# Masks of the first half-sequence added in PSUM, wider idle products and a new order of loads and instructions, in an attention and swish kernel on one core

## The chip, the cores and the metric

The kernel runs on one NeuronCore of a Trainium2 chip. The metric is the device time of one execution in microseconds (us). Before the change the median of three runs is 231.59 us (231.52 to 231.60).

The core has five instruction streams: TensorE (PE in the profile, its weight loads PEld), VectorE (DVE), ScalarE (ACT), GpSimd (POOL) and SyncE (SP), which here only issues DMAs. TensorE writes to PSUM, eight banks of 512 float32 columns on 128 partitions; the other engines bring its results to SBUF.

## The reference

Attention with two kinds of heads, then a layer with w_in, a swish with a factor for each column, and w_out:

```python
rel = pos[:, None] - pos[None, :]
causal = rel >= 0
stream_keep = causal & ((pos[None, :] < 4) | ((rel >= 0) & (rel < 64)))
mask = where(is_retrieval, causal, stream_keep)        # by head
a = softmax(where(mask, q @ k.T / sqrt(64), -1e9))
x = (a @ v) laid out as [3072, 512]                    # 4 batches x 768 rows, 8 heads x 64
h = x @ w_in                                           # [512, 2048]
out = (h * sigmoid(beta * h)) @ w_out                  # [2048, 512]
```

q, k and v are [4, 8, 768, 64] in float32. Heads 0, 2 and 6 are retrieval heads (causal), the others streaming heads (a window of 64 keys and the first 4 keys, the sinks). Inputs are cast to bf16 on the core.

## The kernel before, in words

**Units.** The work is cut into eight half-sequences ("halves") of NQ = 384 rows, two to a batch, numbered n = 0 to 7. Each goes through these stages, whose names are those in the profile:

- q and k are loaded as float32 (tiles `q2f`, `k2f`, 192 KB for a pair of heads; from half 4 on `wf`), cast to bf16 (`c`), transposed on TensorE through `ident` (`b<-ident,c`; six transposes for a pair and half, from half 4 on by DMA) and copied to `QK`. A load of this kind is called a tile below.
- v is loaded in three parts (`vf`, 256 KB each), cast to `vb` and shifted by 64 rows to `vs`.
- Scores go to a PSUM tile `sp` (two tiles of two banks, one step of two heads each); ScalarE takes exp of a whole step to `es` (for two steps of half 0 to a borrowed tile `osb`).
- Masks: after exp, VectorE or GpSimd multiplies `es` by `mask_c` (the causal triangle) or `mask_s` (the streaming window), both 0 or 1.
- Sums (`b<-es,two` and others), their reciprocal, a spread over the partitions (`b<-sc,sel`), the products with V (`sp<-es,vb` and `vs`), and the normalized `xT`, the transposed x.
- w_in: 16 column blocks of 128 for each half, four 384-column products each (`b<-xT,w_in`); ScalarE's tanh to `t`, VectorE's `gT`.
- w_out: three row blocks of 128 for each half, 16 512-column products each (`b<-w_out,gT`), planned in groups of three; copied to `osb` and stored.

w_in and w_out are loaded in four transfers of 1 MB each, through the same three `wf` buffers; each is cast by four casts on GpSimd, one for each column block of w_in or each 128 rows of w_out. `KP` holds keys of the streaming heads gathered from `QK`, nine copies for each half from half 2 on.

**Order.** Nothing is left to a scheduler. `add` (line 137) enters each step, with what it needs and what PSUM banks it takes; the number of a step is its place in the order of these calls. `SEQUENCE` (line 41) lists the step numbers, `CHOICE` (line 97) names the engine of each step that has a choice. `run` (line 147) walks through `SEQUENCE`, works out a planned start from the costs written beside each step, gives each step that takes a buffer the slot that came free first, and emits the steps sorted by planned start. The engines run their instructions in the order of emission and wait on semaphores for one another, so the costs set an order and no time. All instructions are issued from one helper, so the profile gives line 121 for nearly all of them; groups are told apart by tile and shape.

**Idle products.** `FILLS` (line 107) names steps ahead of which TensorE multiplies a cleared operand, or transposes `ident`, that many times (`fill`, line 555) into the bank which the step overwrites; `fill_first` issues 25 at the start. In the profile they are `b<-xT`, `sp<-xT` and `b<-ident`, 128 columns each; there are 25 + 34.

**Loads.** SyncE issues nearly all DMAs in order on one queue. The order before, up to the third transfer of w_out (q0 is the q tile of pair 0; the half stands in brackets; [0] k0 comes from ScalarE's queue; in w_in and w_out the four transfers are numbered 0 to 3):

```
[0] q0 k3 q3 q1 k1 q2, beta, [1] q0 k0, [0] k2, [0] V2 V0 V1, w_in 0, [1] k2 q2 q3 q1 k1 k3,
w_in 1, w_in 2, [1] V0 V1 V2, [2] q1, w_in 3, w_out 3, [2] k1 k2 q0 q2 k0 q3 k3,
w_out 0, w_out 1, [3] k0, w_out 2, [3] q2 k3 q1, [2] V, ...
```

Of the kernel before, what the change touches and what calls it, by code (L numbers as in the profile page):

```python
# [19 lines left out]
NQ = 384  # L20
# [75 lines left out]
]  # L96
CHOICE = (
    "daagaddadadddadaddaddgggdgdddgaaagaggggdaagdddaddadaagddddgaaddgddaaadagdddaddagggggadggdgdgggdgggad"
    "gaadaadaaaadaaaaadaddddaadda"
# [7 lines left out]
FILLS = {28: 8, 45: 5, 32: 1, 51: 7, 36: 1, 54: 5, 60: 1, 24: 4, 76: 2}  # L107
# [19 lines left out]
class _Plan:  # L127

    LAT = {"pe": 0.2, "act": 0.2, "dve": 0.22, "pool": 0.2, "sp": 0.0}

    def __init__(self, rings):
        self.free = {k: [(0.0, i) for i in range(n)] for k, n in rings.items()}
        self.ops, self.refs, self.log, self.where = [], {}, [], {}
        self.same = {}

    def add(self, eng, cost, f, needs=(), gives=(), take=(), drop=(), dma=0.0, mode=None, port=False, begun=(), lat=None, parts=1):

        needs = dict.fromkeys(m for n in needs for m in self.same.get(n, [n]))  # L140
        one = isinstance(eng, str)
        alts = [(eng, cost)] if one else list(zip(eng, cost))
        self.ops.append((0, len(self.ops), dict(alts), (lambda e: f()) if one else f, tuple(needs), tuple(gives),
                         tuple(take), tuple(drop), dma, mode, port, tuple(begun),
                         lat or (2.0 if dma > 0.2 else 3.2), parts))

    def run(self):

        done = {}
        now = {e: 0.0 for o in self.ops for e in o[2]}  # L150
        mode = None
        bus, lock = 1.1, 0.0
# [1303 lines left out]
```

## Time and profile before

| | |
|---|---|
| median of three runs | 231.59 us (231.52 to 231.60) |
| profiled execution: span from the first to the last instruction | 229.49 us |
| granted TensorE clock | 0.999 |
| instructions | 6530 |
| DMA traffic | 42.28 MB, 84264 packets, 66042 of them under 512 B |

The profile is of one execution; it gives the span and no other time for it, so the 2.1 us between span and median are what lies around the instructions. The page has the engines' busy time, the span in 40 slices (busy tenths), the DMA queues, the chain that ended last, the costliest groups and the DMA issues. Lines of the timeline read: start, length, engine, line, operation, tile written and tiles read, shape, count, and in brackets the engine's idle time ahead of it and what ended it. A busy TensorE is not a TensorE at its peak: a row's length holds the pipeline's latency once, so the distance between products is (length - length of one)/(count - 1).

### The profile page before, as it was taken

To read this page: it belongs to the slowest core of one execution; us is meant where nothing else is said; L and a number is where in the kernel's file an instruction comes from. 1 tells how busy PE (TensorE), PEld (TensorE's weight loads), DVE (VectorE), ACT (ScalarE), POOL (GpSimd) and SP (SyncE) were. 2 spreads that over 40 slices of the span, in tenths; PEclk is the share of its full clock that TensorE was granted. 3 is DMA by queue.
4 is the path that set the end of the run, shared out by engine and by line. 5 is a ranking of instruction groups with operands and counts; after the bars stand their busy time and mean duration, and the time that the engine had idled before them with its cause. 6 is when DMAs were issued, how large, how long until landed. Compare 5 with 4: busy or idle time off the path is not lost.

```text
span 229.5 us, 6530 instructions
## 1 busy us (share of the span) xinstructions
PE 222.0 (97%) x2589; PEld 126.8 (55%) x2589; DVE 159.3 (69%) x394; ACT 140.8 (61%) x233; POOL 94.2 (41%) x236
## 2 busy tenths in 40 slices
PE   7699999999999999999999999999999999999995
PEld 6465466664544555464654555745655555456543
DVE  4697988888588957984686687793596459167621
ACT  5799979896076378726894188526857357018610
POOL 5428956964966307559265563048200000000000
PEclk9999999999999999999999999999999999999999
DMA  6999999999989979999999985977300106321012
GB/s 187 274 321 362 237 321 340 375 341 226 220 192 252 213 158 229 270 172 213 250 233 203 209 197 167 192 146 149 101 3 0 50 2 181 105 91 46 3 46 91
DMA packets 84264, 42.28 MB, mean 184 GB/s; under 512 B 66042, under 2 KB 77002, under 8 KB 84234
## 3 DMA queue, kind: packets, MB, share of 16 engines
q1 hardware_dynamic: 83962, 41.67, 74.3%
q8 instruction: 20, 0.33, 0.6%
q10 hardware_dynamic: 272, 0.20, 0.3%
q14 instruction: 10, 0.08, 0.1%
HBM read 32.27 MB, written 6.37 MB: 168 GB/s over the span
## 4 chain that ended last, share of the span: by engine, by line
PE 84%; DMA 4%; ACT 4%; DVE 4%; SPq 1%; issue 1%; ACTq 0%; DVEq 0%
PE b L121 74%; PE sp L121 10%; DMA k2f<-in_k_dram 2%; DMA q2f<-in_q_dram 2%; DVE KP L121 2%; DVE es L121 1%; ACT QK L121 1%; ACT es L121 1%; DVE gT L121 1%; ACT osb L121 1%; SPq L121 1%; ACT c L121 1%; ACT t L121 0%; DVE xT L121 0%; DVE c L121 0%
## 5 line engine op out<-in xcount | busy, mean ns | idle before, releaser
L121 DVE SCALAR_TENSOR_TENSOR gT<-t,b 128x384 bf16<-128x384 f32 x128 | 68.8, 550 | 32.2 <-ACT t L121 28.0
L121 PE MATMUL b<-xT,w_in 128*128 128x384 bf16 x512 | 90.2, 326 | 0.2
L121 PE MATMUL b<-w_out,gT 128*128 128x512 bf16 (+2 forms) x400 | 89.0, 371 | 0.1
L121 ACT ACTIVATE t<-b,beta_h 128x384 f32<-128x384 f32 x128 | 73.0, 585 | 25.1 <-PE b L121 13.7
L121 PEld LDWEIGHTS <-w_in 128*128 128x128 bf16 x512 | 48.7, 98 | 33.9 <-POOL w_in L121 0.6
L121 PEld LDWEIGHTS <-gT 128*128 128x128 bf16 x400 | 37.0, 98 | 40.7 <-issue 1.0
L121 ACT ACTIVATE es<-sp 128x1024 bf16<-128x1024 f32 (+4 forms) x50 | 46.0, 952 | 7.0 <-PE sp L121 7.0
L121 ACT ACTIVATE osb<-b 128x512 f32<-128x512 f32 (+1 forms) x15 | 8.7, 578 | 39.3 <-PE b L121 39.3
L121 POOL CAST c<-wf 128x256 bf16<-128x256 f32 x48 | 18.6, 425 | 12.8 <-DMA wf<-in_k_dram 11.7
L121 POOL COPY KP<-QK 128x24 bf16<-128x24 bf16 (+5 forms) x41 | 9.8, 282 | 22.5 <-DMA QK<-c 13.5
L121 PE MATMUL sp<-QK 64*64 64x64 bf16 (+7 forms) x432 | 16.9, 234 | 1.1 <-ACT QK L121 0.8
L121 DVE TENSOR_SCALAR osb<-b 128x512 f32<-128x512 f32 (+1 forms) x10 | 6.7, 674 | 15.1 <-PE b L121 15.0
L121 DVE TENSOR_TENSOR xT<-sp,R 64x384 bf16<-64x384 f32 (+4 forms) x30 | 16.0, 554 | 1.6 <-PE sp L121 1.0
L121 PEld LDWEIGHTS <-QK 64*64 64x64 bf16 (+1 forms) x432 | 10.9, 105 | 9.8 <-issue 7.4
L121 DVE TENSOR_TENSOR es<-es,mask_c 128x128 bf16<-128x128 bf16 (+3 forms) x42 | 11.9, 308 | 4.2 <-ACT es L121 4.1
L121 DVE TENSOR_TENSOR es<-es,mask_s 128x128 bf16<-128x128 bf16 (+8 forms) x34 | 13.3, 417 | 0.9 <-ACT es L121 0.8
L121 PE MATMUL sp<-es,vb 128*64 128x64 bf16 (+5 forms) x245 | 13.3, 234 | 0.0
L121 POOL CAST vb<-wf 128x512 bf16<-128x512 f32 x18 | 10.8, 611 | 5.9 <-DMA wf<-in_v_dram 5.4
L121 PEld LDWEIGHTS <-vb 128*64 128x64 bf16 x257 | 11.4, 111 | 0.7
L121 DVE COPY QK<-b 128x384 bf16<-128x384 bf16 (+1 forms) x13 | 8.6, 671 | 3.8 <-PE b L121 3.8
L121 POOL COPY vs<-vb 64x512 bf16<-64x512 bf16 x19 | 11.1, 616 | 0.3
L121 POOL CAST w_out<-wf 128x512 bf16<-128x512 f32 x16 | 9.3, 613 | 3.5 <-DMA wf<-in_moe_w_out_dram 3.5
(112 smaller groups left out, 200.4 us busy)
## 6 DMA issues: line engine op xcount, KB each, us to landing
out_dram<-osb SPq DMA_DIRECT2D x23, 256.0 KB, 4.2
wf<-in_v_dram SPq DMA_DIRECT2D x18, 256.0 KB, 4.5
wf<-in_moe_w_in_dram SPq DMA_DIRECT2D x4, 1024.0 KB, 8.4
wf<-in_moe_w_out_dram SPq DMA_DIRECT2D x4, 1024.0 KB
R<-rd SPq DMA_DIRECT2D x9, 384.0 KB, 5.5
q2f<-in_q_dram SPq DMA_DIRECT2D x16, 192.0 KB, 4.5
wf<-in_q_dram SPq DMA_DIRECT2D x12, 256.0 KB, 4.0
wf<-in_k_dram SPq DMA_DIRECT2D x12, 256.0 KB, 4.1
```

Of the source, the lines that this page charges most:

```text
L121: ins = f(*a, **k)
```

## The change

It has these parts:

- For half 0 the masks after exp are gone (`masks_of` gives none). `scores` starts each PSUM bank with products of `ident` and a tile that holds 0 where a score is kept and -1e30 where not (`off_c`, 128 columns, from `mask_c`; `off_s`, 384 columns, from `mask_s`), and the score products add to it. In half 0 that is nine products of 128 columns and five of 384. The two tiles lie in the buffer of the first `xT`, beside the cleared operand, and VectorE forms them with one `tensor_scalar` each. `mask_c` is now made in a step of its own.
- `fill` issues pieces of up to 512 columns, with the cleared operand's first column repeated as moving operand; `FILLS` has four entries, with 16 units of 128 columns instead of 34, beside the 25 of `fill_first`.
- The first transfer of w_in is loaded in two halves, and its four casts may run on VectorE or ScalarE; two are given to VectorE.
- `SEQUENCE` and `CHOICE` are new; steps are emitted in the order of `SEQUENCE` itself, with no planned time, and the PSUM banks come from a list, `SLOTS`.

```diff
-FILLS = {28: 8, 45: 5, 32: 1, 51: 7, 36: 1, 54: 5, 60: 1, 24: 4, 76: 2}
+FILLS = {28: 6, 36: 1, 38: 1, 45: 8}
...
+    def const_off(dst, src):
+        dve.tensor_scalar(out=dst, in0=src, scalar1=-1.0, scalar2=1e30, op0=ADD, op1=MULT)
...
     def fill(dst):
-        for _ in range(held["fill"]):
-            if dst.dtype == BF16:
+        n = held["fill"]
+        if dst.dtype == BF16:
+            for _ in range(n):
                 pe.transpose(dst, ident, ident)
-            else:
-                pe.matmul(dst, blank, blank, start=True, stop=True)
+            return
+        while n:
+            w = min(n, 4)
+            pe.matmul(dst[:, 0:128 * w], blank, blank[:, 0:1].to_broadcast([128, 128 * w]), start=True, stop=True)
+            n -= w
...
+        for i, half in enumerate(rounds[ri] if x.n == 0 else []):
+            if half is None or half[0][0] == "k":
+                continue
+            at = [(0, off_s)] if half[0][0] == "w" else [(c, off_c) for (_, h, kb, c, q0, _) in half if kb * 128 == q0]
+            for j, (c, m) in enumerate(at):
+                pe.matmul(ps[:, i, c:c + m.shape[1]], ident, m, start=j == 0, stop=False, skip_group_check=True)
...
-                    pe.matmul(o[j][0], o[j][1], o[j][2], start=True, stop=True)
+                    pe.matmul(o[j][0], o[j][1], o[j][2], start=x.n > 0, stop=True, skip_group_check=x.n == 0)
...
     def masks_of(pi, ri, n):
         u = n % 2
+        if n == 0:
+            return []
...
-            add("sp", 0.5, lambda s=s, ld=ld: ld(s), dma=2.9, lat=2.1, gives=[("wf", w, s)], begun=[("begun", w, s)],
-                take=[("wf", (w, s), 4)])
+            halves = 2 if (w, s) == ("i", 0) else 1
+            for p in range(halves):
+                add("sp", 0.5, lambda s=s, ld=ld, a=((p, halves) if halves > 1 else ()): ld(s, *a), dma=2.9 / halves, lat=2.1, gives=[("wf", w, s, p)],
+                    needs=[("begun", w, s)] if p else [], begun=[] if p else [("begun", w, s)], take=[] if p else [("wf", (w, s), 4)])
```

The new order of the loads, decoded from `SEQUENCE` in the same notation:

```
beta, [0] q0 q2, [1] k0 q0, [0] q1 k1 k3 q3 k2, [0] V0, [1] q3, [0] V1, [1] k3, [0] V2, [1] q2 q1 k2, w_in 0a,
[1] k1, w_in 0b, w_in 1, [1] V1, w_in 2, [1] V2 V0, [2] q3 q0 q2 k0 k3, w_in 3, [2] k2 q1 k1, [3] q3, w_out 3,
[3] k1 q1, w_out 0, [3] q2 k0 k3 q0, w_out 1, w_out 2, [2] V, ...
```

On TensorE the scores of half 1 come earlier among those of half 0; the transposes of half 2 stand between the last w_in column blocks of half 0 instead of behind them; three of the four transpose steps of half 3 stand before the fourth group of w_out products of half 0; from half 5's w_in on, TensorE's list is the one of before. The `KP` copies of halves 2 and 3 move from VectorE to GpSimd, and the edge masks (`const_edges`) to GpSimd's start.

More of the change, by code (lines that the diff above doesn't have):

```diff
@@ L41 @@
 SEQUENCE = [
[54 rows of a table removed]
[51 rows of a table added]
 ]
 CHOICE = (
[L98 to L99 removed]
+    "aadaagddgdgddaddaaaddgdgaadaggdgaaddaddddaadddddgddddaadddddaaagaddadaagagdddgagdgaddgggdgggagdddggd"
+    "dadadddddadadaddaddddaadda"
+)
+SLOTS = (
+    "0123002131002301021301101023010213101023011030120103210311020312301201103201320132013201012302310120"
+    "1101023011001203120312031102030113102101023010231023102013012100110231002310231023101023201032100131"
+    "02103120013021303012131021023032013201320110321032103210321023023"
 )
@@ L127 @@
 class _Plan:
-    LAT = {"pe": 0.2, "act": 0.2, "dve": 0.22, "pool": 0.2, "sp": 0.0}
     def __init__(self, rings):
-        self.free = {k: [(0.0, i) for i in range(n)] for k, n in rings.items()}
-        self.ops, self.refs, self.log, self.where = [], {}, [], {}
-        self.same = {}
+        self.rings = rings
+        self.ops, self.where, self.same = [], {}, {}
     def add(self, eng, cost, f, needs=(), gives=(), take=(), drop=(), dma=0.0, mode=None, port=False, begun=(), lat=None, parts=1):
@@ L143, in add @@
         self.ops.append((0, len(self.ops), dict(alts), (lambda e: f()) if one else f, tuple(needs), tuple(gives),
-                         tuple(take), tuple(drop), dma, mode, port, tuple(begun),
-                         lat or (2.0 if dma > 0.2 else 3.2), parts))
+                         tuple(take), tuple(drop), dma, mode, port, tuple(begun), lat, parts))
     def run(self):
[L149 to L152, printed above, removed]
@@ L201, in run @@
-        return [x[1:] for x in sorted(order, key=lambda x: x[:2])]
+        choice = iter(CHOICE)
+        engine = {o[1]: {"a": "act", "d": "dve", "g": "pool"}[next(choice)] if len(o[2]) > 1 else list(o[2])[0] for o in self.ops}
+        slots = iter(SLOTS)
+        done, held = set(), {}
+        left = {}
+        assert sorted(SEQUENCE) == list(range(len(self.ops)))
+        for i in SEQUENCE:
+            _, _, _, f, needs, gives, take, drop, *_, begun, _, _ = self.ops[i]
+            assert done.issuperset(needs), (i, set(needs) - done)
+            done.update(gives)
+            done.update(begun)
+            for r, name, refs in take:
+                if r in ("b", "sp"):
+                    slot = r, int(next(slots))
+                    assert slot not in held, (i, slot, held[slot])
+                    held[slot] = name
+                    self.where[r, name] = slot[1]
+                    left[r, name] = refs
+            for key in drop:
+                if key in left:
+                    left[key] -= 1
+                    if not left[key]:
+                        del held[key[0], self.where[key]]
+            yield i, f, engine[i]
@@ L277 @@
     low = consts.tile([128, 1], F32, name="low")
-    blank = xp.tile([128, NP, NQ], BF16, name="xT")[:, 0, 0:128]
+    early = xp.tile([128, NP, NQ], BF16, name="xT")
+    blank, off_s, off_c = early[:, 0, 0:128], early[:, 1, :], early[:, 2, 0:128]
     one = consts.tile([128, 63], BF16, name="one")
@@ L496, in sink_rows @@
         t = bank((2 * b, "k"))
-        fill(t[:, 0:128])
+        fill(t)
         pe.matmul(t[0:96, :], sink_sel, v_b[b][:, 0, :, :].rearrange("p h d -> p (h d)"), start=True, stop=True)
@@ L518, with load_w_in @@
     wst = {}
-    def load_w_in(s):
-        f = stg.tile([128, 2048], F32, name="wf", bufs=RINGS["wf"]).rearrange("p (a n) -> p a n", a=NP)
-        sp.dma_start(out=f, in_=bass.AP(moe_w_in.tensor, moe_w_in.offset + s * 2 * FS, [[d_ff, 128], [128 * d_ff, NP], [1, 2 * FS]]))
-        wst["i", s] = f
+    def load_w_in(s, part=0, parts=1):
+        if part == 0:
+            wst["i", s] = stg.tile([128, 2048], F32, name="wf", bufs=RINGS["wf"]).rearrange("p (a n) -> p a n", a=NP)
+        n = 2 * FS // parts
+        sp.dma_start(out=wst["i", s][:, :, part * n:(part + 1) * n],
+                     in_=bass.AP(moe_w_in.tensor, moe_w_in.offset + s * 2 * FS + part * n, [[d_ff, 128], [128 * d_ff, NP], [1, n]]))
     def load_w_out(s):
@@ L711, in scores @@
         if x.n == 0:
-            fill(ps[:, 0, 0:128])
+            fill(ps[:, 0])
         ops = [[], []]
@@ L881, in sums @@
             if x.n == 0:
-                fill(x.sm[:, 0:128])
+                fill(x.sm)
         byj = [[] for _ in range(TU)]
@@ L1014, in pv @@
         if x.n == 0:
-            fill(o[:, 0, 0:128])
+            fill(o[:, 0])
         ops = [[], []]
@@ L1260, in attention @@
                     drop += [("k2f", (n, "d"))] if ri else []
+                if n == 0:
+                    needs += [("const", "ident")] + [("const", "off" + ("s" if h[0][0] == "w" else "c")) for h in rounds_of(pi, n)[ri] if h and h[0][0] != "k"]
+                    cost += 0.2
                 take.append(("sp", (n, pi, ri), 1))
@@ L1271, in attention @@
             add("pe", cost, lambda bu=bu: [scores(x, pi, ri) for (pi, ri) in bu],
-                needs=needs, gives=gives, take=take, drop=drop, mode=("qk", "sum") if any(h is not None and h[0][0] == "k" for h in rounds_of(*bu[-1][:1], n)[bu[-1][1]]) else "qk")
+                needs=needs, gives=gives, take=take, drop=drop,
+                mode=("qk" if n else None, "sum" if any(h is not None and h[0][0] == "k" for h in rounds_of(*bu[-1][:1], n)[bu[-1][1]]) else "qk"))
             for j, (pi, ri) in enumerate(bu):
@@ L1387 @@
     add("act", 0.2, const_table, needs=[("const", "ident")], gives=[("const", "table")])
-    add("pool", 2.15, const_masks, gives=[("const", "m")])
+    add("pool", 0.55, const_mask_c, gives=[("const", "mc")])
+    add("pool", 1.65, const_masks, needs=[("const", "mc")], gives=[("const", "m")])
+    add("dve", 0.15, lambda: const_off(off_c, mask_c), port=True, needs=[("const", "mc")], gives=[("const", "offc")])
+    add("dve", 0.25, lambda: const_off(off_s, mask_s[0][:, 0:NQ]), port=True, needs=[("const", "mask", 0)], gives=[("const", "offs")])
     add("pool", 0.3, const_two, gives=[("const", "two")])
@@ L1392 @@
         add(("dve", "pool"), (0.3, 0.45), lambda e, u=u: const_mask_new(u, ENG[e]), gives=[("const", "new", u)], port=True,
-            needs=[("const", "edge", u), ("const", "pair")] +[("M", u, pi, ri) for pi in range(NP) for ri in range(len(rounds_of(pi, u))) if mask_cost(pi, ri, u)] + [("const", "mask", 0)])
+            needs=[("const", "edge", u), ("const", "pair")] +[("M", u, pi, ri) for pi in range(NP) for ri in range(len(rounds_of(pi, u))) if mask_cost(pi, ri, u)] + [("const", "mask", 0), ("const", "offs")])
         add("dve", [0.67, 0.3][u], lambda u=u: const_mask_s(u), port=True, needs=[("const", "m")], gives=[("const", "mask", u)])
```

55 lines of the change are left out of this document (5 added, 50 removed), and 105 rows, old and new, of the table SEQUENCE.

## The prediction

> **What bounds the kernel now.** I read the page first: the span, the engines' shares, the DMA slices.
>
> ```profile
> span 229.5 us, 6530 instructions
> PE 222.0 (97%) x2589; PEld 126.8 (55%) x2589; DVE 159.3 (69%) x394; ACT 140.8 (61%) x233; POOL 94.2 (41%) x236
> DMA  6999999999989979999999985977300106321012
> ```
>
> TensorE is busy for 97% of the span, and the DMA engines for nine tenths or more of nearly every slice up to 143 us. An average hides stages, so the second view is the windows.
>
> ```profile
> 0.00:25.00 25.00, 20.73 (x333) 13.98 (x334) 18.24 (x65) 20.63 (x36) 14.08 (x46) 1.00 0.98 291
> 25.00:57.00 32.00, 31.88 (x485) 19.51 (x484) 27.22 (x73) 26.93 (x49) 22.05 (x44) 1.00 1.01 304
> 57.00:225.00 168.00, 167.70 (x1754) 92.03 (x1754) 113.29 (x258) 92.94 (x148) 58.04 (x148) 1.00 0.68 148
> 225.00:229.50 4.50, 1.68 (x21) 1.25 (x19) 0.56 (x1) 0.28 (x1) 0.00 (x0) 0.95 0.27 98
> ```
>
> The first number after the window is its length, the next TensorE's busy time; the last three are clock, DMA share, GB/s. From 25 to 225 us TensorE is idle for 0.12 + 0.30 us. Whatever helps must either let it reach the 25 us mark with more done, or take products away; whatever makes it wait later costs in full. Up to 57 us the DMA queues are full as well (share 1.01), so each load stands where its place in the queue puts it. The third view is TensorE's timeline.
>
> ```profile
> 1.06 2.85 PE L121 MATMUL b<-xT 128*128 128x128 bf16 x25 [1.06 <-DVE xT L121]
> ...
> 4.59 0.51 PE L121 MATMUL b<-ident,c 128*128 128x128 bf16 x6 [0.23 <-ACT c L121]
> ...
> 7.86 0.51 PE L121 MATMUL b<-ident,c 128*128 128x128 bf16 x6 [0.83 <-ACT c L121]
> ...
> 9.63 0.55 PE L121 MATMUL sp<-QK 64*64 64x128 bf16 x20 [0.52 <-ACT QK L121]
> ...
> 19.32 0.48 PE L121 MATMUL b<-xT,w_in 128*128 128x384 bf16 x2
> ...
> 26.09 2.12 PE L121 MATMUL b<-xT,w_in 128*128 128x384 bf16 x12
> 28.15 0.36 PE L121 MATMUL sp<-QK 64*64 64x64 bf16 x14
> ...
> 35.99 2.77 PE L121 MATMUL b<-xT,w_in 128*128 128x384 bf16 x16
> ...
> 43.47 0.83 PE L121 MATMUL b<-ident,c 128*128 128x128 bf16 x12
> ...
> 52.73 3.62 PE L121 MATMUL b<-w_out,gT 128*128 128x512 bf16 x16
> ```
>
> The first 25 rows of work are idle products, 0.106 us apart (2.85 - 0.2 us over 25); warm, a 128-column product takes (0.83 - 0.22)/11 = 0.055 us, a 384-column one (2.77 - 0.33)/15 = 0.163, a 512-column one (3.62 - 0.38)/15 = 0.216. The first product with w_in is at 19.32, the last four w_in columns of half-sequence 0 are at 35.99, the first w_out product at 52.73.
>
> **The change, part by part.** *Masks.* Six mask steps of half-sequence 0 leave VectorE and GpSimd.
>
> ```profile
> L121 DVE TENSOR_TENSOR osb<-osb,mask_s 128x768 bf16<-128x768 bf16 x2 | 1.1, 554 | 0.3 <-ACT osb L121 0.3
> ...
> 9.36 1.16 POOL L121 TENSOR_TENSOR es<-es,mask_c 128x512 bf16<-128x512 bf16 x1 [0.88 <-ACT es L121]
> ...
> 14.29 0.67 POOL L121 TENSOR_TENSOR es<-es,mask_c 128x256 bf16<-128x256 bf16 x1 [2.11 <-ACT es L121]
> ```
>
> In their place stand nine 128-column and five 384-column products, 9 x 0.055 + 5 x 0.163 = 1.31 us of TensorE. They lie before 16 us, where TensorE waits for loads and casts between products (rows at 7.86 and 9.63), so I cost them at 0; without that cover they cost 1.31 us. The step removed ended at 14.96, but the sums' reciprocal did not wait for it:
>
> ```profile
> 8.75 1.02 DVE L121 COPY QK<-b 128x384 bf16<-128x384 bf16 x2
> ...
> 14.68 1.36 DVE L121 COPY vs<-vb 64x1024 bf16<-64x1024 bf16 x3
> ...
> 15.96 0.55 DVE L121 RECIPROCAL b<-b 96x64 f32<-96x64 f32 x1
> ```
>
> VectorE was shifting V until 16.04. V is what is late next: in the new order two q/k tiles stand between the three V loads. The price of a load comes from casts that waited for one:
>
> ```profile
> 6.88 0.51 ACT L121 CAST c<-q2f 128x384 bf16<-128x384 f32 x1 [1.26 <-DMA q2f<-in_q_dram]
> ...
> 10.01 0.72 DVE L121 CAST c<-k2f 128x384 bf16<-128x384 f32 x1 [0.24 <-DMA k2f<-in_k_dram]
> ...
> 26.61 2.41 POOL L121 CAST w_in<-wf 128x512 bf16<-128x512 f32 x4 [0.27 <-DMA wf<-in_moe_w_in_dram]
> ...
> 29.68 0.92 POOL L121 CAST vb<-vf 128x512 bf16<-128x512 f32 x1 [0.66 <-DMA vf<-in_v_dram]
> ...
> 33.47 1.93 POOL L121 CAST w_in<-wf 128x512 bf16<-128x512 f32 x3 [1.85 <-DMA wf<-in_moe_w_in_dram]
> ...
> 38.01 0.61 POOL L121 CAST w_out<-wf 128x512 bf16<-128x512 f32 x1 [1.59 <-DMA wf<-in_moe_w_out_dram]
> ...
> 47.38 1.73 POOL L121 CAST w_out<-wf 128x512 bf16<-128x512 f32 x3 [0.36 <-DMA wf<-in_moe_w_out_dram]
> 50.68 2.84 POOL L121 CAST w_out<-wf 128x512 bf16<-128x512 f32 x5 [1.57 <-DMA wf<-in_moe_w_out_dram]
> ```
>
> Five q/k tiles landed between the first two rows: 3.13/5 = 0.63 us each. Three V loads landed between 26.6 and 29.7: 1.02 each. The last V load of half 0 then lands at 10.0 + 3 x 1.02 + 2 x 0.63 = 14.3 us, 1.3 later than three V loads back to back. With its cast (0.6 to 0.9), the shift (0.6) and a copy that now stands ahead of it (0.51, row 8.75), the reciprocal starts near 16.4 instead of 15.96.
>
> *Idle products.* Counted in 128 columns, 59 become 41, in 512-wide pieces. They fill waits, and I cost their loss at 0. The first now waits for mask_c and a subtraction on VectorE, since both stand ahead of the clearing of its operand, and GpSimd forms mask_c before the identity.
>
> ```profile
> 1.12 0.65 POOL L121 TENSOR_SCALAR_AFFINE_SELECT ident<-ident 128x128 bf16<-128x128 bf16 x2
> ...
> 2.48 0.33 POOL L121 TENSOR_SCALAR_AFFINE_SELECT mask_c<-mask_c 128x128 bf16<-128x128 bf16 x1
> ```
>
>
> ```profile
> 7.55 0.50 POOL L121 CAST c<-k2f 128x384 bf16<-128x384 f32 x1 [3.10 <-DMA k2f<-in_k_dram]
> ```
>
> That is a memset, one such row of 0.33 and the subtraction: some 0.7 us, so the warming starts near 1.8 instead of 1.06. The first transposes wait for loads and casts until 4.59 (row above), and beta's load now stands ahead of theirs; 25 products in 2.65 us end before that. The edge masks also move to GpSimd's start, where it waited 3.10 us for a load. So 0.
>
> Here a page speaks against the change. The Trainium skill, TensorE: Matmul & The Clock Gate, "Part 1: The HAM clock gate", says that the array runs at half rate until about 3.4 us of sustained work and falls back after an idle window of that length. The trace agrees with the first half (0.106 against 0.055 us). No row here has TensorE idle so long, so no run here shows the second; it is a rival below.
>
> *Order.* I decoded the new list: each number is one planned step. In the old order the first w_in product came 19.32 - 15.96 = 3.36 us after the reciprocal; in the new one a q cast (up to 0.72, row 10.01) and a copy (0.51) also stand on VectorE between them: 16.4 + 3.4 to 4.6, near 20.3. But TensorE is not idle for it: the scores of half 1 stand earlier. At the sixth w_in step of half 0 (26.09 in the old order) one score step more is behind it, that of the row at 28.15, 0.29 us to the next product. If the sixth step starts at 26.1 as before, the lead is 0.3; if VectorE keeps pace, up to 0.8 more, 1.1. None of it enters the sum, since TensorE then meets two loads.
>
> First, w_in's fourth megabyte. It was the second load behind half 1's V, and is now the sixth: four tiles more, 4 x 0.63 = 2.5, lands at 33.4 + 2.5 = 35.9. GpSimd's casts of it (0.56 to 0.6 each, rows 26.61 and 50.68) now alternate with three q/k casts:
>
> ```profile
> 43.84 0.51 POOL L121 CAST c<-q2f 128x384 bf16<-128x384 f32 x1
> 44.29 0.51 POOL L121 CAST c<-k2f 128x384 bf16<-128x384 f32 x1
> ```
>
> 0.45 each. The fourth w_in cast ends at 35.9 + 4 x 0.58 + 3 x 0.45 = 39.6, and the last column's four products near 40.4. Before, they ended at 35.99 + 2.77 = 38.8; but the new order then also has four groups of six transposes of half 2 behind it (4 x 6 x 0.055 = 1.3), which the old one did later: equal work at 40.1. I take 0, between 0 and 0.5.
>
> Second, w_out's third megabyte. Six more tiles stand ahead of it: between the rows 47.38 and 50.68 one tile and a megabyte took 3.3 us, and six tiles take 6 x 0.55 to 0.63. It lands at 50.6 + 3.5 = 54.1 (53.2 to 55). Its four casts end at 54.1 + 4 x 0.56 = 56.3, and the fourth group of three w_out products needs all four. In the old order that group starts at 52.73 + 9 x 0.216 = 54.7; with three groups of transposes of half 3 moved ahead of it (3 x 0.33), 55.7. The wait: 56.3 - 55.7 = 0.6; between 0 (lands early) and 1.6.
>
> *KP copies.* Half 3's nine copies move from VectorE to GpSimd.
>
> ```profile
> 64.18 3.78 DVE L121 COPY KP<-QK 128x360 bf16<-128x360 bf16 x9 [1.05 <-ACT QK L121]
> ```
>
> ```profile
> 67.62 0.21 PE L121 MATMUL sp<-QK,KP 64*64 64x24 bf16 x5
> 68.02 0.20 PE L121 MATMUL sp<-QK,KP 64*64 64x24 bf16 x3 [0.19 <-DVE KP L121]
> ```
>
> These held TensorE for 0.36 us: 0.40 between the two rows, less some 0.04 for the products themselves. On GpSimd they stand further ahead of the scores that need them: -0.36; between -0.4 and 0. Half 2's copies move too, ahead of w_out casts; GpSimd had 0.36 and 1.57 us of waiting for loads there (rows 47.38, 50.68), which hides them.
>
> *The rest of the order.* From half 5 on, TensorE's order is the same list. Between 57 and 225 us TensorE's idle sum is 0.30 us; the order there can give back at most about that and some switching, and lose as much as any wait: -0.7 to +1.0, taken as 0. The w_in load in two halves only splits one transfer: 0.
>
> **Sum.** Span 229.5 + 0.6 - 0.36 = 229.7 or 229.8. The page has no time but the span; the median of the runs, 231.59, lies 2.1 above it, which I keep: 231.9 us. By the bounds of all terms, the masks' 1.31 among them, it is 230.2 to 235.8; the ends need every term at its end.
>
> **Rivals.**
>
> *The lead survives.* A transfer need not wait for all that stand ahead of it: w_out's first landed 4.5 us after the w_in megabyte issued just before it (rows 33.47, 38.01), where a megabyte and a tile else took 3.3, so transfers issued later moved beside it. If w_in and w_out land 1 to 2 us earlier than counted, nothing waits, and the lead of up to 1.1 us and the 0.36 stay: 231.6 - 1.5 = 230.1. For it: the waits forecast are short beside that. Against it: the DMA share is full, and more bytes stand ahead.
>
> *The queue jams behind V (slower).* An issue can hang:
>
> ```profile
> 20.27 5.97 SPq L121 DMA_DIRECT2D vf<-in_v_dram  x1
> ```
>
> Here one V issue held the queue for 5.97 us. Now five tiles and w_in's fourth megabyte stand behind three V loads and two megabytes of weights. If that hold grows with what is queued, every load after it is late, and both waits for weights grow, by 0.8 each if it grows by a seventh: 231.9 + 1.6 = 233.5. It decides once the fourth w_in megabyte lands after 36.5. For it: the row. Against it: the hold ended when queued bytes had drained, and those are no more than before.
>
> *A cold clock.* With 18 fewer idle products the array could fall back to the pace of the first 25 between 6 and 16 us. The mask products would take 1.31 us more, and transposes and scores as much again (rows at 4.59, 7.86, 9.63, 0.5 each); if half of some 3 us has no cover, 231.9 + 1.5 = 233.4. Against it: the longest wait there is 0.83. The page named above is the rule behind this case.
>
> *The change doesn't do what it says.* The lists, the PSUM banks' among them, only name an order; if the waits are those of before, masks and fills move nothing: 231.6.
>
> **Chances.** Forecast 0.40 (own range 231.1 to 232.7); lead 0.28; jam 0.24; cold clock 0.04; no effect 0.04. A difference under 0.2% (0.46 us) can't be told from none here. Faster: 0.28 + 0.04 of the forecast's = 0.32. Same: 0.22 + 0.04 = 0.26. Slower: 0.24 + 0.04 + 0.14 = 0.42. The range reaches into both neighbours: 229.7 to 233.9.
>
> **What would show it.** GpSimd's first cast of w_in's fourth group should start near 36, and w_out's third near 54, each ending a wait for a load; TensorE should wait between 54 and 57 us for about 0.6, and no more for KP near 68. The windows should give TensorE in 0 to 25 us a higher share. If no cast waits near 36 and 54 and TensorE has no wait there, the forecast is wrong on the fast side; if the issue of a V load holds the queue longer than 6 us and the waits reach 2 us, on the slow side. Scores of half 0 at half their pace would show the cold clock.

## The result, and the profile after

The changed kernel takes 234.46 us (median of four runs, 233.62 to 235.62), the kernel before beside it 231.56 us (231.26 to 231.60). The ratio is 1.0126, with a 95% interval from 1.0091 to 1.0160: slower by 2.9 us, 0.56 us above the range's upper end. The profiled execution took 234.17 us with a span of 232.5. Ratios below are to the kernel before in the same comparison; e11 and e14 have none, because too few of their executions were undisturbed, and the traces of e4, e8, e11 and e14 are of disturbed executions, so that only the places of their waits are read from them.

The page of the changed kernel, the three lines that answer to those of before:

```profile
span 232.5 us, 6441 instructions
PE 220.7 (95%) x2540; PEld 124.7 (54%) x2561; DVE 159.2 (68%) x397; ACT 137.6 (59%) x226; POOL 89.9 (39%) x230
DMA  6999999999896998999999989965300105421012
```

Its windows, with the columns named in the prediction:

```profile
0.00:25.00 25.00, 20.19 (x314) 11.86 (x315) 18.46 (x68) 19.21 (x33) 14.26 (x51) 1.00 1.01 283
25.00:57.00 32.00, 31.05 (x461) 19.47 (x455) 26.76 (x57) 27.15 (x51) 25.33 (x52) 1.00 1.03 311
57.00:225.00 168.00, 164.94 (x1739) 90.52 (x1758) 112.69 (x272) 90.92 (x144) 50.36 (x128) 1.00 0.69 147
225.00:232.50 7.50, 4.54 (x37) 2.84 (x35) 1.25 (x2) 0.28 (x1) 0.00 (x0) 1.00 0.19 70
```

The clock is 1.00 throughout. TensorE's idle time from 25 to 57 us rises from 0.12 to 0.95 us, and the end moves from 229.5 to 232.5. The third row overstates idle time: 19 matmul records are missing there (1739 against 1758 weight loads). So I went by another measure, the **lag**: how much later than in the kernel before TensorE had issued the same number of useful columns, masks and idle products left out. It is worked out from the start of every product (of a missing one, from its weight load); a plus is late.

| time in the kernel before | 26 us | 35 | 40 | 46 | 56 | 71 | 82 | 86 | 117 | 126 | 157 to the end |
|---|---|---|---|---|---|---|---|---|---|---|---|
| changed kernel | +0.33 | +1.06 | +1.79 | +1.40 | +1.85 | +1.22 | +1.22 | +1.92 | +1.81 | +2.78 | +2.86 |
| the same again (e0) | +0.27 | +1.14 | +2.56 | +2.38 | +2.88 | +2.25 | +2.25 | +2.37 | +2.98 | +3.66 | +3.71 |

Two limits. Between 26 and 61 us the two lists issue different products, so the marks there are rough: without the transposes in the count, those at 40 and 56 us are 0.75 and 0.86 higher. And a lag compares two single executions: e13 and e17 below, whose front is the old one, lag by 0.6 us at 26 us all the same.

Three places stand out: 31 to 40 us, 84 us, 124 us. The first is the largest: 0.9 us from 26 to 71 us, 2.0 in e0. The next three fences are the changed kernel's timelines of TensorE, GpSimd and VectorE at these places and at the marks that the prediction named:

```profile
1.74 2.85 PE L123 MATMUL b<-xT 128*128 128x512 bf16 x7 [1.74 <-DVE xT L123]
...
21.76 0.66 PE L123 MATMUL b<-xT,w_in 128*128 128x384 bf16 x3
...
38.22 0.82 PE L123 MATMUL b<-xT,w_in 128*128 128x384 bf16 x4 [0.68 <-POOL w_in L123]
...
84.84 6.86 PE L123 MATMUL b<-xT,w_in 128*128 128x384 bf16 x40 [0.54 <-DVE osb L123]
...
124.87 5.17 PE L123 MATMUL b<-w_out,gT 128*128 128x512 bf16 x21 [0.53 <-DVE gT L123]
```

```profile
15.04 0.61 POOL L123 CAST vb<-vf 128x512 bf16<-128x512 f32 x1 [2.37 <-DMA vf<-in_v_dram]
...
37.55 1.17 POOL L123 CAST w_in<-wf 128x512 bf16<-128x512 f32 x2 [2.17 <-DMA wf<-in_moe_w_in_dram]
...
51.91 2.29 POOL L123 CAST w_out<-wf 128x512 bf16<-128x512 f32 x4 [0.24 <-DMA wf<-in_moe_w_out_dram]
```

```profile
16.65 0.56 DVE L123 RECIPROCAL b<-b 96x64 f32<-96x64 f32 x1
...
84.09 0.69 DVE L123 TENSOR_SCALAR osb<-b 128x512 f32<-128x512 f32 x1 [2.10 <-DMA out_dram<-osb]
...
122.36 0.80 DVE L123 COPY vs<-vb 64x1024 bf16<-64x1024 bf16 x1 [1.55 <-POOL vb L123]
```

The next two fences are SyncE's DMA queue, first of the kernel before, then of the changed one (start of an issue and its length):

```profile
28.16 0.42 SPq L121 DMA_DIRECT2D wf<-in_moe_w_in_dram  x1
...
71.74 0.36 SPq L121 DMA_DIRECT2D out_dram<-osb  x1
72.20 4.74 SPq L121 DMA_DIRECT2D wf<-in_v_dram  x3
```

```profile
30.28 1.23 SPq L123 DMA_DIRECT2D wf<-in_moe_w_in_dram  x1
...
73.35 4.79 SPq L123 DMA_DIRECT2D wf<-in_v_dram  x3
78.24 1.18 SPq L123 DMA_DIRECT2D out_dram<-osb  x1
```

*31 to 40 us.* w_in's fourth megabyte is issued 2.1 us later and is in flight for 7.3 us (30.28 to the cast at 37.55) instead of 5.3 (28.16 to 33.47). GpSimd waits 2.17 us for it, TensorE for GpSimd. *84 us.* VectorE's copy to `osb` waits 2.10 us for a store that now stands behind three V loads (78.24) instead of ahead of them (71.74), and TensorE waits 0.54 us for the copy. *124 us.* A shift of V waits 1.55 us for its cast and stands ahead of the `gT` that w_out's products need: 0.53 us. TensorE's timeline of e0, the changed kernel again, has the first and the third of these waits, none at 84 us, and one near 109 us that the trace above has not:

```profile
38.99 0.82 PE L123 MATMUL b<-xT,w_in 128*128 128x384 bf16 x4 [1.36 <-POOL w_in L123]
...
109.17 0.81 PE L123 MATMUL b<-xT,w_in 128*128 128x384 bf16 x4 [0.69 <-DVE osb L123]
...
125.75 5.17 PE L123 MATMUL b<-w_out,gT 128*128 128x512 bf16 x22 [0.32 <-DVE gT L123]
```

So the wait for w_in belongs to the order; where TensorE waits later is in part the chance of one execution.

### The profile page after: what moved, and what is told of

It is laid out like the page before. It is cut to its first block, busy times and chain, and to the rows that moved or that the text cites. A ratio compares the mean times of both kernels' runs of the same rounds, so it can differ in the third digit from the quotient of the medians.

```text
span 232.5 us, 6441 instructions
## 1 busy us (share of the span) xinstructions
PE 220.7 (95%) x2540; PEld 124.7 (54%) x2561; DVE 159.2 (68%) x397; ACT 137.6 (59%) x226; POOL 89.9 (39%) x230
## 4 chain that ended last, share of the span: by engine, by line
PE 72%; DMA 16%; POOL 3%; SPq 2%; DVE 2%; ACT 2%; issue 1%; DVEq 0%; ACTq 0%; POOLq 0%
PE b L123 64%; DMA wf<-in_moe_w_in_dram 8%; PE sp L123 7%; DMA out_dram<-osb 2%; SPq L123 2%; DMA vf<-in_v_dram 2%; DMA wf<-in_k_dram 2%; DMA k2f<-in_k_dram 2%; DVE gT L123 1%; POOL w_in L123 1%; POOL c L123 1%; ACT es L123 1%; DVE vs L123 1%; ACT t L123 1%; POOL vb L123 1%
## 5 line engine op out<-in xcount | busy, mean ns | idle before, releaser
L123 ACT ACTIVATE t<-b,beta_h 128x384 f32<-128x384 f32 x128 | 71.8, 582 | 36.8 <-PE b L123 23.1
L123 PE MATMUL b<-w_out,gT 128*128 128x512 bf16 (+2 forms) x379 | 85.7, 370 | 2.6 <-issue 1.3
L123 PEld LDWEIGHTS <-w_in 128*128 128x128 bf16 x512 | 48.6, 98 | 36.5 <-issue 1.9
L123 POOL COPY KP<-QK 128x24 bf16<-128x24 bf16 (+5 forms) x57 | 15.4, 317 | 23.4 <-DMA QK<-c 22.8
L123 ACT ACTIVATE osb<-b 128x512 f32<-128x512 f32 (+1 forms) x9 | 5.1, 562 | 30.8 <-PE b L123 30.8
L123 DVE TENSOR_SCALAR osb<-b 128x512 f32<-128x512 f32 (+1 forms) x16 | 10.8, 678 | 18.2 <-PE b L123 16.1
L123 PE MATMUL sp<-QK 64*64 64x64 bf16 (+6 forms) x432 | 17.1, 234 | 0.4 <-ACT QK L123 0.4
L123 DVE COPY vs<-vb 64x1536 bf16<-64x1536 bf16 (+4 forms) x19 | 11.1, 587 | 4.8 <-POOL vb L123 4.5
L123 DVE TENSOR_TENSOR es<-es,mask_c 128x128 bf16<-128x128 bf16 (+2 forms) x42 | 11.0, 286 | 4.6 <-ACT es L123 4.6
L123 POOL CAST w_in<-wf 128x512 bf16<-128x512 f32 x14 | 8.7, 647 | 4.6 <-DMA wf<-in_moe_w_in_dram 4.6
L123 PE MATMUL b<-ident,c 128*128 128x128 bf16 x96 | 8.2, 220 | 2.3 <-DVE c L123 1.1
```

The lines of the kernel that those rows point to most:

```text
L123: ins = f(*a, **k)
```

## The experiments

**My theory** was the late load: TensorE's new list wants w_in's fourth megabyte and all eight q/k tiles of half 2 (1.5 MB) before half 1's first column, where the old list had only one pair's two tiles of half 2 ahead of it and put half 1's columns before the other six. So 1.2 MB more must land by the same point, on queues that are full. **The rivals:** the mask products lie on TensorE's path and are paid in full; the late waits (84 and 124 us) are the loss; the moved `KP` copies or the fewer idle products cost it.

### The changed kernel again, and the masks alone (e0, e1)

e0 has no edit. e1 is the kernel before with one part of the change:

```diff
 (kernel before, its order of loads and instructions)
-masks of half 0 after exp, on VectorE and GpSimd
+masks of half 0 as products of ident with off_c, off_s ahead of the scores
+idle products in pieces of up to 512 columns, 59 units as before
```

> The changed kernel itself once more, beside the others: 234.5, between 233.6 and 235.6, with TensorE waiting near 37, 84 and 124 us again if these waits belong to the order (theory A); if they come from the chance of one execution, they stand elsewhere.

> The lists of the kernel before (order, engines, PSUM banks, transfers) with half 0's masks put into PSUM and as many idle columns as before, in pieces of up to 512. Theory A (the order of the lists costs the time: loads, a store and a shift of V that stand too late or too early): the mask products are hidden in the first 25 us, so 231.6, between 231.2 and 232.1. Theory B (the mask products are on the path, 1.31 us of TensorE before the 25 us mark and nothing to give it back): 232.9, between 232.5 and 233.3.

e0: 234.66 us, 1.0112 [1.0068, 1.0155]; of the three waits expected, the one at 84 us is not in its trace (above). e1: 232.45 us, 1.0026 [0.9996, 1.0055], which is 0.6 us, with an interval from -0.1 to 1.3. Its trace lags by 0.98 us from 26 us on and by 1.05 at the end. VectorE's and TensorE's timelines of e1:

```profile
16.56 0.55 DVE L126 RECIPROCAL b<-b 96x64 f32<-96x64 f32 x1
```

```profile
20.45 0.48 PE L126 MATMUL b<-xT,w_in 128*128 128x384 bf16 x2
```

The reciprocal is 0.6 us later than before (15.96), the first w_in product 1.1 (19.32). But in e13 and e17, with the old masks, that product stands at 19.9 and the lag at 26 us is 0.6. So 0.4 to 0.6 us are left for the masks in the old order, the interval of the times holds zero as well, and they are not the 2.9 us.

### The masks taken out (e2, e11)

e2 is the changed kernel without the mask products (diff), e11 the old order without any mask step of half 0.

```diff
-        for i, half in enumerate(rounds[ri] if x.n == 0 else []):
...
-                    pe.matmul(o[j][0], o[j][1], o[j][2], start=x.n > 0, stop=True, skip_group_check=x.n == 0)
+                    pe.matmul(o[j][0], o[j][1], o[j][2], start=True, stop=True)
```

> The changed kernel without half 0's mask products: half 0's scores stay unmasked, the 1.31 us of TensorE are left out, all else is as in the changed kernel. Theory A: at most 0.4 us less than the changed kernel's 234.5, so 234.1 to 234.5. Theory B: the whole 1.31 us less, 233.2.

> The order of the kernel before with half 0's masks left out altogether, in PSUM and as multiplies (half 0's scores stay unmasked). Beside the run with masks in PSUM in that order (1.0026 of the kernel before) it prices the mask products: if they were hidden, as predicted, the same, 232.0; if they stand on the path between the scores and the reciprocal, 0.6 to 1.0 less, 231.1 to 231.5, or less still if the multiplies of the kernel before were on it too.

e2: 239.36 us, 1.0353 [1.0301, 1.0405]. Less work, and some 5 us more. The reason is in TensorE's timeline and in the windows of e2 (clock third from the right):

```profile
10.95 0.61 PE L123 MATMUL b<-ident,c 128*128 128x128 bf16 x6 [1.75 <-DVE c L123]
```

```profile
9.00:12.00 3.00, 1.15 (x15) 0.75 (x14) 1.30 (x5) 2.30 (x4) 0.50 (x1) 1.00 1.12 248
12.00:15.00 3.00, 2.50 (x41) 1.53 (x38) 2.04 (x6) 2.88 (x6) 1.17 (x4) 0.64 1.05 270
15.00:18.00 3.00, 3.00 (x82) 1.99 (x80) 1.65 (x4) 2.62 (x5) 1.90 (x6) 0.50 0.89 250
```

After one wait of 1.75 us, in a stretch with 1.15 us of work in three, the clock is halved until 19.7 us. The changed kernel had 2.15 us of work in that stretch and kept its clock. The prediction's cold clock exists, then, though not in the changed kernel: its mask products also serve as idle products. A second fall, from 40.2 to 47.0 us, comes at the end of a wait of 3.82 us with no releaser in the trace. Neither run gives a price of the masks: e11 (237.43 us, five runs) got a wait of 2.55 us at 35.98 with no releaser in the trace and new waits near 62 us.

### The load put earlier (e3)

```diff
-[2] q3 q0 q2 k0 k3, w_in 3, [2] k2 q1 k1
+[2] q3, w_in 3, [2] q0 q2 k0 k3 k2 q1 k1
```

> The changed kernel with one load moved: w_in's fourth megabyte second behind half 1's V, as in the kernel before, instead of sixth. Theory A: its casts start near 34 to 35 us instead of 37.55, TensorE's wait at 37.2 us (0.84) goes, and the time falls by 0.8 to 1.0, to 233.6. Theory B: TensorE is late anyway and finds the next wait, so less than 0.3 changes.

236.61 us, 1.0201 [1.0157, 1.0245]: worse than the changed kernel. TensorE no longer waits for w_in, but for half 2's tiles. Timeline and windows of e3:

```profile
37.07 0.34 PE L126 MATMUL b<-ident,c 128*128 128x128 bf16 x3 [2.55 <-POOL c L126]
38.17 0.50 PE L126 MATMUL b<-ident,c 128*128 128x128 bf16 x3 [0.76 <-POOL c L126]
```

```profile
35.00:38.00 3.00, 0.34 (x3) 0.17 (x3) 0.31 (x1) 1.00 (x3) 1.81 (x4) 0.89 1.04 296
38.00:41.00 3.00, 2.83 (x37) 2.12 (x38) 0.96 (x1) 0.23 (x1) 3.00 (x7) 0.50 1.03 360
```

0.34 us of work in three, then half the clock. Both are wanted by the same point, so the order between them only chooses which one is late.

### The load left out (e12, and e13 in the old order)

The edit is the same in both. TensorE's instructions all stay.

```diff
+        if s == 3:
+            wst["i", 3] = wst["i", 2]
+            return
```

> The changed kernel without the load of w_in's fourth megabyte: columns 12 to 15 of every half are cast from the third megabyte, so the output is another. The casts stay. Theory A (debt of the DMA queues between 33 and 43 us): TensorE's wait near 37 us goes, everything loaded later lands some 3 us earlier, and the time falls by 1.0 to 2.5 us: 232.2 to 233.6. Theory B (the front or the order of the engines costs the time, not the loads): less than 0.4 changes, 234.3 or more.

> The control: the kernel before with the same load left out and the same columns cast from the third megabyte. TensorE is idle for only 0.12 us between 25 and 57 us there, so both theories expect no change, 231.5, between 231.2 and 231.7; what it gains all the same is to be taken off from the gain of the changed kernel.

e12: 232.54 us, 1.0047 [1.0028, 1.0067]. Of the 1.26% (e0: 1.12%) 0.5% are left; 1.5 to 1.8 us are gone (with the two intervals, give or take some 1 us). The edit takes a megabyte off the queues altogether, so this is the price of the load in this order, and not of its late place alone. GpSimd casts at 34.58 without a wait:

```profile
34.58 1.17 POOL L123 CAST w_in<-wf 128x512 bf16<-128x512 f32 x2
```

Four fences show the same two windows, 35 to 38 and 38 to 41 us, for the kernel before, the changed kernel, e0 and e12; the number after the length is TensorE's busy time.

```profile
35.00:38.00 3.00, 3.00 (x31) 1.93 (x27) 1.93 (x5) 2.92 (x9) 1.41 (x3) 1.00 1.08 358
38.00:41.00 3.00, 2.88 (x21) 1.69 (x20) 2.75 (x7) 2.67 (x5) 2.57 (x9) 1.00 1.08 332
```

```profile
35.00:38.00 3.00, 2.44 (x46) 1.57 (x41) 2.38 (x7) 2.42 (x6) 0.83 (x2) 1.00 1.07 353
38.00:41.00 3.00, 2.67 (x28) 1.93 (x29) 2.09 (x5) 2.19 (x6) 3.00 (x7) 1.00 1.05 366
```

```profile
35.00:38.00 3.00, 2.63 (x54) 1.85 (x49) 2.61 (x7) 2.34 (x6) 0.27 (x1) 1.00 0.99 327
38.00:41.00 3.00, 1.97 (x15) 1.23 (x16) 1.43 (x3) 1.51 (x4) 2.68 (x6) 1.00 1.03 323
```

```profile
35.00:38.00 3.00, 2.93 (x49) 2.06 (x47) 2.93 (x7) 2.71 (x7) 3.00 (x7) 1.00 0.92 265
38.00:41.00 3.00, 2.89 (x30) 2.02 (x29) 2.64 (x7) 2.83 (x5) 0.88 (x3) 1.00 1.07 377
```

TensorE's idle time in these six microseconds is 0.12, 0.89, 1.40 and 0.18 us: with the load gone it is back at the old figure. e12's lag is -0.12 us at 26, +0.50 at 46, +0.19 at 71 and +0.50 at the end; its profiled execution was the fastest of twelve (231.71), so the end says less than the median. From 26 to 71 us, where both lists have issued the same products again, the lag grows by 0.9 us in the changed kernel, 2.0 in e0 and 2.5 each in e6 and e7 (both below), all four with the load, and by 0.3 and 0.4 in e12 and e16 without it.

The control e13, meant to be neutral, is not: 235.23 us, 1.0144 [1.0120, 1.0167]. With less to load, GpSimd starts half 3's casts at 53.94 instead of 56.76 us, beside VectorE's masks. VectorE's timeline in the kernel before, then in e13, then TensorE's in e13:

```profile
53.63 0.69 DVE L121 TENSOR_TENSOR es<-es,mask_s 128x256 bf16<-128x256 bf16 x3
```

```profile
55.00 1.61 DVE L121 TENSOR_TENSOR es<-es,mask_s 128x256 bf16<-128x256 bf16 x3
```

```profile
57.66 0.19 PE L121 MATMUL b<-es,one_z 128*32 128x64 bf16 x1 [0.63 <-DVE es L121]
58.27 0.19 PE L121 MATMUL b<-es,one_z 128*32 128x64 bf16 x1 [0.41 <-DVE es L121]
59.16 0.21 PE L121 MATMUL b<-es,one_z 128*32 128x64 bf16 x2 [0.71 <-DVE es L121]
```

The same three masks take 1.61 us instead of 0.69, and TensorE waits 1.75 us in three pieces. The windows of e13 show the clock behind it:

```profile
57.50:60.00 2.50, 1.22 (x30) 0.62 (x30) 2.50 (x10) 0.00 (x0) 2.38 (x6) 0.96 0.45 86
60.00:62.50 2.50, 2.44 (x10) 0.90 (x7) 1.09 (x3) 0.48 (x1) 1.98 (x9) 0.50 0.03 5
```

So e12 shows what the load costs in the new order only as far as nothing like this moved there; its lag after 46 us shows nothing of the kind.

### The late waits (e6, e16)

```diff
 SyncE:    the store of half 1's first row block ahead of half 4's V loads
 VectorE:  two shifts of half 6's V behind the gT steps of half 3's last columns
```

e6 is the changed kernel with these two moves; e16 is e12 with them.

> The changed kernel with two steps moved: the first store of half 1 stands ahead of half 4's V loads on SyncE instead of behind them, and half 6's two shifts of V stand behind the last swish of half 3 on VectorE instead of between its last three. Theory A: the waits of 0.7 near 84 us and 0.7 + 0.25 near 124 us go: 234.5 - 1.7 = 232.9, between 232.5 and 233.4. Theory B: TensorE meets another wait for every one that goes, so less than 0.4 changes.

> The changed kernel without the load of w_in's fourth megabyte (columns 12 to 15 cast from the third, another output), and with the two late steps moved: the first store of half 1 ahead of half 4's V loads, half 6's shifts of V behind the last swish of half 3. Without the load alone 232.5 was measured, and its trace had one late rise of the lag left, 0.6 near 124 us. Theory A: that goes, 231.9, between 231.5 and 232.2. Theory B (the late steps are not what costs): 232.5.

e6: 234.29 us, 1.0110 [1.0071, 1.0150]. e16: 232.66 us, 1.0062 [1.0039, 1.0085], no better than e12. Neither trace has the waits at 84 and 124 us, and both have another near 108. TensorE's timeline of e6 (its stage wait included), then of e16:

```profile
39.48 0.82 PE L126 MATMUL b<-xT,w_in 128*128 128x384 bf16 x4 [2.18 <-POOL w_in L126]
...
108.98 0.81 PE L126 MATMUL b<-xT,w_in 128*128 128x384 bf16 x4 [0.42 <-DVE osb L126]
```

```profile
107.37 0.81 PE L126 MATMUL b<-xT,w_in 128*128 128x384 bf16 x4 [0.48 <-DVE osb L126]
```

It isn't shown that the new wait replaces the old ones: e0, with nothing moved, has it too and has none at 84 us. What the times show is that moving the two steps gave nothing that can be measured. By the intervals of e0 and e6, a gain of up to some 1.4 us isn't excluded, the 1.7 expected is; by those of e12 and e16, at most some 0.4 us.

### KP and the idle products (e7, e17, e10)

```diff
 e7  (changed kernel)  the KP copies of halves 2 and 3 that moved: GpSimd to VectorE
 e17 (kernel before)   the same copies: VectorE to GpSimd
 e10 (changed kernel)  idle products as before: 59 units, each of 128 columns
```

> The changed kernel with the KP copies of halves 2 and 3 back on VectorE, at the same places of the order. The prediction put this move at -0.36, so giving it back costs 0.36: 234.9; between 234.5 (the copies are hidden on either engine) and 235.2 (0.6, the fall of the lag between 61 and 71 us, is all theirs).

> The kernel before with the KP copies of halves 2 and 3 on GpSimd, every engine's order otherwise the same. The prediction's step: TensorE's hold of 0.36 near 67.7 us goes, 231.1. The other view, from the changed kernel with the copies back on VectorE, which made no difference: the place in the order counted and not the engine, so 231.5; more than that if the copies on GpSimd take longer or stand in front of casts that TensorE waits for.

> The changed kernel with the idle products as in the kernel before: 59 of 128 columns each, at the same steps. The prediction costed the fewer ones at nothing: 234.6, between 234.2 and 235.0, unless they stand in the way of useful products. If fewer idle products let the clock fall in the changed kernel (the cold clock), this one is faster; the granted clock of 1.0 in its traces speaks against that.

e7: 234.74 us, 1.0163 [1.0118, 1.0208]; the hold near 68 us is gone, though the copies are on VectorE again. It is gone in e1 too, which has the old lists and the old engine for KP, but a TensorE that comes 1 us later. So the engine isn't needed for it: the place in the lists, or lateness alone, is enough. e17: 231.52 us, 1.0001 [0.9984, 1.0018]; the trace has no hold near 67.7 us, and the time is that of before (-0.4 to +0.4 us). e10: 235.78 us, 1.0170 [1.0131, 1.0209], clock 1.00; more idle products don't help.

### Old and new orders put together (e4, e5, e8, e9, e14, e15)

Each takes the list of one kernel up to a point and the other's from there.

```diff
 e4   new up to half 0's sixth w_in step, old after it
 e5   new up to the first w_out product, old after it
 e8   old up to half 2's first w_in step, new after it
 e9   old up to half 0's fourth w_in step, new after it
 e14  new, but the loads and steps of half 2's and 3's tiles in the old order
 e15  e14 with e6's two moves
```

> The changed kernel's lists up to the fifth w_in column of half 0 (some 26 us: masks in PSUM, idle products, loads in the new order), then the steps that are left in the order of the kernel before, on its engines. Theory A (late loads, a store and a shift in the order behind 26 us cost the time): the lag at 26 us was 0.3 to 0.4 in the changed kernel's trace and nothing is added, so 231.9, between 231.5 and 232.3. Theory B (the front, masks and idle products, costs it): near the changed kernel's 234.5.

> The changed kernel's lists up to the first w_out product (52 us), then the order of the kernel before. Theory A: the lag at 52 us in the changed kernel's traces, 1.5 (1.5 to 2.5), stays, and neither the wait of the store near 84 us nor that of the shift near 124 us comes: 233.0 to 233.6, with the wait for w_in's fourth megabyte near 37 us still there. Theory B: as the changed kernel, 234.5.

> The order of the kernel before, with half 0's masks in PSUM, up to the first w_in column of half 2 (some 80 us), then the changed kernel's order. Old order with masks in PSUM alone gave 1.0026 of the kernel before, 232.1. Theory A (the changed order behind 80 us loses on its own account, by a store behind V loads and a shift of V between swishes, 1.4 to 1.6 in the two traces of the changed kernel): 233.5, between 233.1 and 233.9. Theory B (these waits are only what an already late order meets): 232.1.

> The order of the kernel before, with half 0's masks in PSUM, up to the fifth w_in column of half 0 (26 us), then the changed kernel's order; w_in's fourth megabyte is thereby loaded early. Theory A, made sharper (between 33 and 43 us the changed order needs w_in's fourth megabyte and all eight q/k tiles of half 2 before half 1's first column, the order before only two of the tiles: some 1.2 MB more, so TensorE waits whichever is loaded first): a wait of 1 to 3 us near 35 to 38 us for half 2's casts, and 234.5 to 236.5. Theory B (what is lost there comes from the new front): no such wait and at most 233.5.

> The changed kernel with one stage in the order of the kernel before: the loads, casts, transposes, copies, scores and masks of halves 2 and 3, w_in's fourth megabyte and all of w_out stand at the old places among the w_in and w_out products; front, products and everything from 60 us on as in the changed kernel. Theory A: no wait at 37 us, the lag stays at 0.4 to 0.8 up to 60 us, the two late waits stay: 232.8 to 233.6. Theory B: as the changed kernel, 234.6. New waits at the seams are possible, and the trace will name them.

> As the run with the old tile stage, and the two late steps moved as well (the first store of half 1 ahead of half 4's V loads, half 6's shifts of V behind the last swish of half 3). Theory A: 0.7 to 1.5 less than that run: 231.6 to 232.4, within 0.4 of the kernel before. Theory B: as the changed kernel, 234.6.

| | us | ratio | a new wait of TensorE |
|---|---|---|---|
| e4 | 237.31 | 1.0230 [1.0193, 1.0268] | 1.64 us for `es` at 33.2 |
| e5 | 234.72 | 1.0139 [1.0099, 1.0178] | 1.23 us for `es` at 60.70 |
| e8 | 236.55 | 1.0181 [1.0135, 1.0228] | 2.40 us for `gT` at 94.74 |
| e9 | 238.32 | 1.0299 [1.0268, 1.0330] | 0.89 us for `c` at 39.33, six for `gT` (1.8 in all) |
| e14 | 246.07 | | 5.37 us for `gT` at 63.66 |
| e15 | 246.51 | 1.0635 [1.0603, 1.0667] | 5.05 us for `gT` at 61.77 |

All are slower than both kernels or no faster than the changed one, each with a wait near its seam that neither parent has. They divide nothing. In e5 the wait for w_in stays (0.92 us at 38.59) and those at 84 and 124 us are gone, but its seam cost as much, so it can't be read either way.

## Why the prediction was wrong, point by point

**The step that failed** is the fourth megabyte in "Order": "lands at 33.4 + 2.5 = 35.9 ... I take 0, between 0 and 0.5". In the changed kernel it landed at 37.55 and in e0 at 38.32, and TensorE waited 0.68 and 1.36 us for its casts (e6, with the same front: 38.81 and 2.18). The shift counted for four tiles was 2.5; the cast came 4.1 later (37.55 - 33.47), 2.1 of it a later issue and 2.0 a longer flight. My sum priced the tiles by the pace of landings and had no term for a flight that grows; why it grew was not tried. Behind the size stands a thing not asked: what the bound engine's list wants by each point. The transposes appear in my sum as 1.3 us of work that "the old one did later", not as eight tiles that must land first. e12 puts the price of the load in this order at 1.5 to 1.8 us, give or take 1. That the tiles' place makes it so dear is argued, from e3 above all: e14, meant to test it, made larger waits of its own.

- *Masks, 0; 1.31 without cover.* The cover may have been thinner: e1 says 0.6 us (-0.1 to 1.3), its trace 0.4 more than the two other traces of the old front. The products lie between loads, but the reciprocal moved with them.
- *V and the reciprocal.* V landed near 14.9 (14.3 forecast), the reciprocal started at 16.65 (16.4). About right; but the first w_in product, forecast near 20.3, came at 21.76.
- *The lead of 0.3 to 1.1 at the sixth w_in step.* Not seen, and its sign is open: the changed kernel lags by 0.33 there (e0 0.27), but e6, e7 and e12, with the same front, are 0.1 to 0.2 ahead of the trace of before, and e13 and e17, with the old front, 0.6 behind it. TensorE's busy time in the first 25 us, expected to rise from 20.73, was 20.19 us, in e0 21.20. So the loss comes after 26 us.
- *w_out's third megabyte, 0.6.* No wait: it was there at 51.9 instead of 54.1, and TensorE was late already.
- *KP, -0.36.* The hold is gone, but e17 shows no gain from that (-0.4 to +0.4 us, with 0.36 at the edge).
- *The rest, 0, between -0.7 and +1.0.* In the trace +1.6 from 71 us on (e0 1.5), outside. But e6 and e16 got nothing measurable back, so it can't be booked as a term of its own.
- *First idle products* at 1.74 us (1.8 forecast): right, and free.
- *The sum.* The bounds of its terms add up to 230.5 and 236.0, not to 230.2 and 235.8. And of the 2.1 us between span and median, 1.7 lie around the instructions (234.17 against 232.5 for one execution); the rest was between executions.

**The rivals.** The lead survives: no, w_in didn't land earlier than counted but later. The jam: its time (233.5) is the nearest, and its point of decision (a landing after 36.5) was passed; its mechanism is absent, since no V issue held the queue for longer than before (4.60 us for two at 20.10; before, 5.97 for one). Slower, but for another reason. The cold clock: not here; e2, e3 and e13 have it.

**What stays open.** The 0.5% that e12 leaves: masks (e1's 0.6 us would be half of it), late waits, or the order elsewhere. No run took the masks out without a colder clock or a new wait.

## What to carry to other kernels

In an order fitted to the arrival of loads, add up by every point of the bound engine's list the bytes that it wants by then, and compare with what the queues can land; a load's place in the queue says only half of it. If two loads are wanted at the same point, exchanging them moves the wait and doesn't remove it (in e3 it grew). And a wait in one trace is not yet a price: of the changed kernel's three, a second execution had two, and a fourth elsewhere (e0), and moving the steps behind the late ones gave nothing measurable (e6, e16).

## What the runs showed of the hardware

- TensorE's clock fell to half after waits below three microseconds: 1.75 us in e2, 1.75 in three pieces in e13, 2.55 in e3, where a stretch of 2.5 to 3 us had 0.34 to 1.22 us of work (in e2 and e3 all of it transposes, in e13 none). It stayed so for some 3.4 us in e13 and 6.8 in e2. With 2.15 us of work in three, the changed kernel kept its clock. The Trainium skill, TensorE: Matmul & The Clock Gate, "Part 1: The HAM clock gate", gives an idle window of about 3.4 us for the fall; these three falls came without so long an idle time, so here the measurements decide: a wait half as long, with little work around it, was enough in e2. The fall at the end of e2's 3.82 us agrees with the page.
- VectorE's masks (two inputs from SBUF) took 0.54 us each beside GpSimd's casts instead of 0.23 (e13). The Trainium skill, GPSIMD Engine Reference, "1. Specifications", says that both share SBUF interfaces when VectorE has two SBUF inputs; the trace agrees.
- TensorE stood still for 3.82 us in e2 (to 41.03) and 2.55 us in e11 with no releaser in the trace. Why was not tried.
